# Re-planning an interleaved attention and gated-FFN kernel: plan constants, cut layer norms, the residual add on VectorE, v loads issued from GpSimd

## Chip, cores and metric

The kernel runs on one core of one Trainium2 chip. The metric is device time in microseconds (us) of one execution. f1, f2, f3 and b5 were timed on another chip than the other experiments, each beside the kernel before; across rounds the ratios to that kernel are the fair comparison. A number called *excess* is used throughout: the starts of all matmuls are taken from the trace, and from each distance between two neighbours the streaming time is taken off (0.216 us for 512 columns, 0.056 us for 128; unrounded 0.2159 and 0.0557). What is left is time in which TensorE was waiting or half clocked. A distance is put down to the later of its two matmuls.

## The reference

Two layers, each a sliding-window attention (32 heads of 32, window of 8 keys two positions apart) and a gated feed-forward part, over 2048 tokens of width 1024 in bf16:

```python
x = A_x
x = x + attn(layernorm(x), A_wqkv, A_wo)      # softmax over 8 dilated keys per query
x = x + ffn(layernorm(x), B_w1, B_w3, B_w2)   # silu(x@w1) * (x@w3) @ w2, F = 3584
x = x + attn(layernorm(x), A_wqkv, A_wo)      # same weights again
x = x + ffn(layernorm(x), B_w1, B_w3, B_w2)
```

## The kernel before

The tokens are cut into four chunks of 512. For each chunk and layer there are pieces of work: the layer norm, 24 QKV projections ("Q", 8 matmuls each), 16 products q*k on VectorE ("P"), each followed by a small reduction over the head dimension on TensorE ("R", 4 matmuls of 128 columns), a softmax ("S"), 16 weighted sums over v on VectorE ("V"), the output projection ("W"), then gate and up projections ("GU") and the down projection ("W2"). A planner in the kernel gives each piece a length, goes through time, and emits the pieces in the order of its plan; the engines then take their instructions in program order.

```python
T_LN, LAT_LN = 7.8, 4.5     # a layer norm is one block of 7.8 us on VectorE
LAT_QP = 7.0                # from a projection's end to the first product that uses it
LAT_VW = 9.0                # from the attention's end to its output projection
...
def ln_emit(c):             # one block: statistics, power, normalise, transpose, four times
    for j in range(4):
        ...  nc.vector.bn_stats ... nc.gpsimd.tensor_tensor(pow) ... nc.vector.scalar_tensor_tensor
        nc.scalar.activation(out=xn[:], in_=xc[:, j, :], func=ACTF.Identity, scale=rstd[:], bias=nmr[:])
        for kt in range(KT):
            nc.tensor.transpose(tp[:, kt, :], xn[:, P * kt:P * (kt + 1)], ident[:])
        nc.scalar.copy(out=xnT[:, :, P * j:P * (j + 1)], in_=tp[:])
...
def vl_emit():              # v loads: 4 DMAs, one buffer, issued by SyncE
    for j in range(4):
        nc.sync.dma_start(out=v2[32 * j:32 * (j + 1), :, :], in_=...)
...
def w_emit(n, j):           # output projection; the residual comes in by an identity matmul
    for ft in range(NFT):
        nc.tensor.matmul(ps[:], lhsT=oT[...], rhs=wo_sb[...], start=(ft == 0), stop=False)
    nc.tensor.matmul(ps[:], lhsT=ident[:], rhs=xs, start=False, stop=True)
    nc.scalar.copy(out=xs, in_=ps[:])
```

## Time and profile before

| | before |
|---|---|
| median of 6 runs | 1786.07 us (1782.42 to 1786.47) |
| span of the profiled run | 1780.7 us |
| matmuls, and their pure streaming | 8512, 1673.7 us |
| before the first matmul / after the last | 10.0 / 6.0 us |
| excess | 90.8 us, of it 42.2 between 120 and 360 us |

The slices of the page, the stretches and the order of matmuls near 280 us are shown in the prediction below. TensorE's waits over the whole span (total us, times, longest), first row:

```profile
PE Lps L306 <- DVE prod L290: 33.6, 17, 3.4
```

`Lps` is the accumulator of the reductions R and `prod` the VectorE product that each needs.

### The profile page before, as it was taken

The numbers are of one execution on the slowest core, as the hardware profiler recorded it, in microseconds if no ns is written. First come the engines' busy times: TensorE is split into PE (matmuls) and PEld (weight loads), VectorE is DVE, ScalarE is ACT, GpSimd is POOL, SyncE is SP. The second block draws the span as 40 slices with busy tenths as digits, with TensorE's granted clock in tenths as the row PEclk, the third lists the DMA queues.
The fourth block names the chain that finished last, engine by engine and source line by source line (L and its number), as shares of the span: only waits on it lengthen the run. The fifth ranks groups of instructions, "written<-read, shape, count | busy, mean of one in ns | idle before, by whom it ended". The sixth has DMA issues, their size and how long they took to land.

```text
span 1780.7 us, 21604 instructions
## 1 busy us (share of the span) xinstructions
PE 1698.8 (95%) x8512; PEld 812.4 (46%) x8512; DVE 1083.5 (61%) x1669; ACT 569.0 (32%) x855; POOL 41.5 (2%) x82
## 2 busy tenths in 40 slices
PE   6998994999999999999999999999999999999998
PEld 3544542444444444444444445444454444444443
DVE  5685599965688456925678256783278733333334
ACT  5442430422322334223342334322342233222221
POOL 2000000100000000000000000000000000000000
PEclk9999996999999999999999999999999999999999
DMA  9979496366346387563965459554694635546452
GB/s 298 242 234 234 149 265 144 98 169 196 97 142 170 115 249 175 148 166 126 256 166 146 139 165 238 160 167 127 206 246 131 188 112 173 153 142 189 144 160 76
DMA packets 453622, 307.13 MB, mean 172 GB/s; under 512 B 92048, under 2 KB 419728, under 8 KB 453520
## 3 DMA queue, kind: packets, MB, share of 16 engines
q1 hardware_dynamic: 453520, 305.75, 60.9%
q8 instruction: 66, 1.08, 0.3%
q14 instruction: 36, 0.29, 0.1%
HBM read 267.49 MB, written 38.22 MB: 172 GB/s over the span
## 4 chain that ended last, share of the span: by engine, by line
PE 80%; DVE 13%; DMA 3%; ACT 2%; issue 1%; POOL 0%; SPq 0%; DVEq 0%; ACTq 0%; POOLq 0%
PE mm L433 20%; PE mm L429 20%; PE mm L459 18%; PE mm L214 14%; PE mm L390 5%; DVE prod L286 3%; DVE prod L290 2%; DMA k<-Kd 2%; DVE pvtd L362 2%; DVE o L363 2%; PE tp L180 1%; DMA Kd<-qkvb 1%; PE Lps L306 1%; DVE acc L466 1%; DVE stats L168 1%
## 5 line engine op out<-in xcount | busy, mean ns | idle before, releaser
L429 PE MATMUL mm<-xnT,wb 128*128 128x512 bf16 x1792 | 424.8, 379 | 2.2 <-DVE acc L466 2.1
L433 PE MATMUL mm<-xnT,wb 128*128 128x512 bf16 x1792 | 424.2, 379 | 0.0
L459 PE MATMUL mm<-wb,hT 128*128 128x512 bf16 x1792 | 401.3, 380 | 11.2 <-DVE acc L466 9.8
L214 PE MATMUL mm<-xnT,wb 128*128 128x512 bf16 x1536 | 347.9, 382 | 4.0 <-ACT qkvb L216 4.0
L439 DVE TENSOR_TENSOR hT<-ub,sg 128x512 bf16<-128x512 bf16 x224 | 94.4, 422 | 376.1 <-ACT ub L438 376.1
L436 ACT ACTIVATE sg<-mm 128x512 bf16<-128x512 f32 x224 | 134.0, 598 | 500.5 <-PE mm L429 487.7
L459 PEld LDWEIGHTS <-hT 128*128 128x128 bf16 x1792 | 174.7, 98 | 220.7 <-issue 16.5
L433 PEld LDWEIGHTS <-wb 128*128 128x128 bf16 x1792 | 175.1, 98 | 209.9
L429 PEld LDWEIGHTS <-wb 128*128 128x128 bf16 x1792 | 173.9, 98 | 205.9 <-issue 3.2
L468 DVE TENSOR_TENSOR acc<-mm,acc 128x512 f32<-128x512 f32 x320 | 213.5, 686 | 65.4 <-PE mm L459 64.6
L214 PEld LDWEIGHTS <-wb 128*128 128x128 bf16 x1536 | 163.5, 109 | 157.8 <-issue 9.3
L286 DVE TENSOR_TENSOR prod<-q,k 128x2048 bf16<-128x2048 bf16 x128 | 153.4, 1218 | 131.3 <-DMA k<-Kd 85.9
L438 ACT CAST ub<-mm 128x512 bf16<-128x512 f32 x224 | 131.2, 586 | 239.8 <-PE mm L433 239.7
L216 ACT CAST qkvb<-mm 128x512 bf16<-128x512 f32 x192 | 111.8, 587 | 250.3 <-PE mm L214 247.3
L363 DVE TENSOR_TENSOR o<-o,pvtd 128x2048 bf16<-128x2048 bf16 x112 | 136.6, 1220 | 1.9
L362 DVE TENSOR_TENSOR pvtd<-attn,v 128x2048 bf16<-128x2048 bf16 x112 | 136.6, 1219 | 1.4
L290 DVE TENSOR_TENSOR prod<-prod 128x1024 bf16<-128x1024 bf16 (+1 forms) x256 | 131.4, 550 | 1.6
L390 PE MATMUL mm<-wo_sb,oT 128*128 128x512 bf16 x512 | 122.2, 382 | 0.0
L168 DVE BATCH_NORM_STATS2 stats<-x 128x6 f32<-128x512 bf16 x128 | 84.4, 673 | 43.0 <-ACT x L393 40.8
L177 ACT ACTIVATE xn<-x,nmr,rstd 128x1024 bf16<-128x1024 bf16 x64 | 79.9, 1251 | 47.6 <-DVE nmr L174 35.6
L306 PE MATMUL Lps<-prod,Zsel 128*128 128x128 bf16 x512 | 48.4, 228 | 33.9 <-DVE prod L290 33.6
L390 PEld LDWEIGHTS <-oT 128*128 128x128 bf16 x512 | 50.2, 99 | 59.5 <-issue 2.2
(39 smaller groups left out, 507.1 us busy)
## 6 DMA issues: line engine op xcount, KB each, us to landing
wb<-in_B_w_dram SPq DMA_DIRECT2D x336, 512.0 KB, 4.3
wb<-in_A_wqkv_dram SPq DMA_DIRECT2D x96, 512.0 KB, 5.1
v<-Vd SPq DMA_DIRECT2D x32, 284.0 KB, 6.3
k<-Kd SPq DMA_DIRECT2D x16, 526.0 KB, 4.5
Qd<-qkvb SPq DMA_DIRECT2D x16, 512.0 KB, 4.4
q<-Qd SPq DMA_DIRECT2D x16, 512.0 KB, 4.2
Kd<-qkvb SPq DMA_DIRECT2D x16, 512.0 KB, 4.4
Vd<-qkvb SPq DMA_DIRECT2D x16, 512.0 KB, 5.2
```

The source lines that it names most:

```text
L214: nc.tensor.matmul(ps[:], lhsT=wb[:, kt % (KT // 2), c_lo:c_hi:c_st], rhs=st["xnT"][:, kt, :], start=(kt == 0), stop=(kt == KT - 1))
L286: nc.vector.tensor_tensor(out=prod[:], in0=in0, in1=in1, op=ALU.mult)
L290: nc.vector.tensor_tensor(out=prod[:, 0:g], in0=prod[:, 0:g], in1=prod[:, g:2 * g], op=ALU.add)
L362: nc.vector.tensor_tensor(out=tmp[:], in0=a_b, in1=vv, op=ALU.mult)
L363: nc.vector.tensor_tensor(out=o2[:, dsl, :], in0=o2[:, dsl, :], in1=tmp[:], op=ALU.add)
L390: nc.tensor.matmul(ps[:], lhsT=oT[:, ft, P * j:P * (j + 1)], rhs=wo_sb[:, ft, 512 * n:512 * (n + 1)], start=(ft == 0), stop=False)
L429: nc.tensor.matmul(g_ps[:], lhsT=w1b[:, kt, lo:lo + P], rhs=xnT[:, kt, :], start=(kt == 0), stop=(kt == KT - 1))
L433: nc.tensor.matmul(u_ps[:], lhsT=w3b[:, kt, lo:lo + P], rhs=xnT[:, kt, :], start=(kt == 0), stop=(kt == KT - 1))
L436: nc.scalar.activation(out=sg[:], in_=g_ps[:], func=ACTF.Silu)
L438: nc.scalar.copy(out=ub[:], in_=u_ps[:])
L459: nc.tensor.matmul(ps[:], lhsT=hT[:, fi, P * j:P * (j + 1)], rhs=w2b[:, fi % 2, 512 * n:512 * (n + 1)], start=(k == 1), stop=(k == nmm))
L468: nc.vector.tensor_tensor(out=ac, in0=ps[:], in1=ac, op=ALU.add)
```

## The change

The intent is to have TensorE wait less early on and to take work from it. Five things are done at once: two latencies of the plan are raised, the layer norm is cut into twelve pieces (four of each kind) that the planner places singly, with the transposes' TensorE time now in the plan (its own plan constants and two small buffers change with it), the residual is added by VectorE, the v loads are issued from GpSimd, and layer norms are kept in the order of their stages. Cut to its core:

```diff
+V2_DMA = "gpsimd"
+LN_SPLIT = False
+A3_RES_PE = False
+W2_INTERLEAVE = False
-T_LN = 7.8
-LAT_LN = 4.5
-LAT_QP = 7.0
+T_LN = 1.95
+LAT_LN = 1.5
+LAT_QP = 13.0
-LAT_VW = 9.0
+LAT_VW = 25.0
...
-    def ln_emit(c):
+    def build_ln(name, c, st, x_deps):
+        def stats_emit(j): ...
+        def norm_emit(j): ...
+        def tr_emit(j): ...
+        for j in range(4):
+            sp_ = Pc(f"LN {name} {j}", "dve", T_LN, ...)
+            np_ = Pc(f"LNn {name} {j}", "pe", 0.0, ...)
+            tp_ = Pc(f"LNt {name} {j}", "pe", KT * T_MM128 + 0.1, ...)
...
-                nc.sync.dma_start(out=v2[32 * j:32 * (j + 1), :, :],
+                v2_dma.dma_start(out=v2[32 * j:32 * (j + 1), :, :],
...
-            nc.tensor.matmul(ps[:], lhsT=ident[:], rhs=xs, start=False, stop=True)
-            nc.scalar.copy(out=xs, in_=ps[:])
+                nc.vector.tensor_tensor(out=xs, in0=ps[:], in1=xs, op=ALU.add)
...
+        if i > 0:
+            stg[2].deps.append((stages[i - 1][2], 0.0))
```

The three flags that are off leave the corresponding parts as they were.

More of the change, by code (lines that the diff above doesn't have):

```diff
@@ L25 @@
 T_MM128 = 0.057
-T_LN = 7.8
-LAT_LN = 4.5
-LAT_QP = 7.0
+T_LN = 1.95
+LAT_LN_POW = 1.4
+LAT_LN_NRM = 1.4
+LAT_LN = 1.5
+LAT_QP = 13.0
 MARGIN_R = 2.0
-LAT_VW = 9.0
+LAT_VW = 25.0
 T_SOFTMAX = 5.6
@@ L120 @@
     nc.sync.dma_start(out=wo_sb[:], in_=A_wo.rearrange("(ft p) n -> p ft n", p=P))
+    v2_dma = {"sync": nc.sync, "gpsimd": nc.gpsimd, "scalar": nc.scalar}[V2_DMA]
     def load_w(src_ap, shape):
@@ L159, in xnt_free, with stats_emit @@
         return None if rel.end is None else rel.end + 0.3
-    def ln_emit(c):
-        xc = x_c[c]
-        xnT = work.tile([P, KT, CH], BF16, name="xnT", tag="xnT", bufs=XNT_BUFS)
-        for j in range(4):
+    def build_ln(name, c, st, x_deps):
+        def stats_emit(j):
+            if j == 0:
+                st["xnT"] = work.tile([P, KT, CH], BF16, name="xnT", tag="xnT", bufs=XNT_BUFS)
+            xc = x_c[c]
             stats = small.tile([P, 2, 6], F32, name="stats", tag="stats", bufs=3)
@@ L169, in ln_emit @@
             nc.vector.bn_aggr(out=mv[:], in_=stats[:])
-            rstd = small.tile([P, 1], F32, name="rstd", tag="rstd", bufs=3)
-            nmr = small.tile([P, 1], F32, name="nmr", tag="nmr", bufs=3)
+            rstd = small.tile([P, 1], F32, name="rstd", tag="rstd", bufs=4)
+            nmr = small.tile([P, 1], F32, name="nmr", tag="nmr", bufs=4)
             nc.vector.tensor_scalar_add(out=rstd[:], in0=mv[:, 1:2], scalar1=EPS)
@@ L175, in ln_emit, with norm_emit, tr_emit @@
                                            op0=ALU.mult, op1=ALU.mult)
+            st[("ln", j)] = (rstd, nmr)
+        def norm_emit(j):
+            rstd, nmr = st.pop(("ln", j))
             xn = work.tile([P, D], BF16, name="xn", tag="xn", bufs=2)
-            nc.scalar.activation(out=xn[:], in_=xc[:, j, :], func=ACTF.Identity, scale=rstd[:], bias=nmr[:])
+            nc.scalar.activation(out=xn[:], in_=x_c[c][:, j, :], func=ACTF.Identity, scale=rstd[:], bias=nmr[:])
+            st[("xn", j)] = xn
+        def tr_emit(j):
+            xn = st.pop(("xn", j))
             tp = psum.tile([P, KT, P], BF16, name="tp", tag="tp", bufs=1)
@@ L180, in ln_emit @@
                 nc.tensor.transpose(tp[:, kt, :], xn[:, P * kt:P * (kt + 1)], ident[:])
-            nc.scalar.copy(out=xnT[:, :, P * j:P * (j + 1)], in_=tp[:])
-        return xnT
+            nc.scalar.copy(out=st["xnT"][:, :, P * j:P * (j + 1)], in_=tp[:])
+        first = prev_s = prev_t = None
+        for j in range(4):
+            deps = list(x_deps) if j == 0 else [(prev_s, 0.0)]
+            sp_ = Pc(f"LN {name} {j}", "dve", T_LN, lambda j=j: stats_emit(j), deps=deps,
+                     extra=(xnt_free if j == 0 else None))
+            dve_urg.append(sp_)
+            np_ = Pc(f"LNn {name} {j}", "pe", 0.0, lambda j=j: norm_emit(j),
+                     deps=[(sp_, LAT_LN_POW if LN_SPLIT else 0.0)])
+            pe_small.append(np_)
+            tdeps = [(np_, LAT_LN_NRM if LN_SPLIT else 0.0)] + ([(prev_t, 0.0)] if prev_t is not None else [])
+            tp_ = Pc(f"LNt {name} {j}", "pe", KT * T_MM128 + 0.1, lambda j=j: tr_emit(j), deps=tdeps)
+            pe_small.append(tp_)
+            first = first or sp_
+            prev_s, prev_t = sp_, tp_
+        return first, prev_t
     QKV_BLOCKS = ((0, 0), (1, 0), (0, 1), (1, 1), (2, 0), (2, 1))
@@ L189, in build_attn @@
         st = {}
-        ln = Pc(f"LN A{li}.{c}", "dve", T_LN, lambda: st.__setitem__("xnT", ln_emit(c)), deps=x_deps, extra=xnt_free)
-        dve_urg.append(ln)
+        ln, ln_done = build_ln(f"A{li}.{c}", c, st, x_deps)
         big = []
@@ L235, in build_attn @@
                 p = Pc(f"Q A{li}.{c} b{bi}.{fi}", "pe", KT * T_MM, lambda bi=bi, fi=fi: q_emit(bi, fi),
-                       deps=[(ln, LAT_LN)] if (bi == 0 and fi == 0) else [], wloads=wl)
+                       deps=[(ln_done, LAT_LN)] if (bi == 0 and fi == 0) else [], wloads=wl)
                 big.append(p)
@@ L259, in vl_emit @@
                 vbase = Vt[0:1, col:col + 1].offset
-                nc.sync.dma_start(out=v2[32 * j:32 * (j + 1), :, :],
-                                  in_=bass.AP(Vt.tensor, vbase, [[vpitch, D], [1, P + HALO]]))
+                v2_dma.dma_start(out=v2[32 * j:32 * (j + 1), :, :],
+                                 in_=bass.AP(Vt.tensor, vbase, [[vpitch, D], [1, P + HALO]]))
             st["v2"] = v2
@@ L390, in w_emit @@
                 nc.tensor.matmul(ps[:], lhsT=oT[:, ft, P * j:P * (j + 1)], rhs=wo_sb[:, ft, 512 * n:512 * (n + 1)],
-                                 start=(ft == 0), stop=False)
-            nc.tensor.matmul(ps[:], lhsT=ident[:], rhs=xs, start=False, stop=True)
-            nc.scalar.copy(out=xs, in_=ps[:])
+                                 start=(ft == 0), stop=(ft == NFT - 1 and not A3_RES_PE))
+            if A3_RES_PE:
+                nc.tensor.matmul(ps[:], lhsT=ident[:], rhs=xs, start=False, stop=True)
+                nc.scalar.copy(out=xs, in_=ps[:])
+            else:
+                nc.vector.tensor_tensor(out=xs, in0=ps[:], in1=xs, op=ALU.add)
             if n == 1 and j == 3:
@@ L400, in build_attn @@
                 deps = [(lastv, LAT_VW)] if lastw is None else [(lastw, 0.0)]
-                lastw = Pc(f"W A{li}.{c} {n}.{j}", "pe", (NFT + 1) * T_MM, lambda n=n, j=j: w_emit(n, j), deps=deps)
+                lastw = Pc(f"W A{li}.{c} {n}.{j}", "pe", (NFT + (1 if A3_RES_PE else 0)) * T_MM,
+                           lambda n=n, j=j: w_emit(n, j), deps=deps, dve_cost=(0.0 if A3_RES_PE else 0.78))
                 pe_small.append(lastw)
-        return big, lastw
+        return big, lastw, ln
     def build_ffn(last, c, x_deps):
         st = {}
-        ln = Pc(f"LN B{int(last)}.{c}", "dve", T_LN, lambda: st.__setitem__("xnT", ln_emit(c)), deps=x_deps,
-                extra=xnt_free)
-        dve_urg.append(ln)
+        ln, ln_done = build_ln(f"B{int(last)}.{c}", c, st, x_deps)
         groups = [list(range(g0, min(g0 + FB_GROUP, NFB))) for g0 in range(0, NFB, FB_GROUP)]
@@ L482, in build_ffn, with mk_gu, mk_w2 @@
         gu_last = {}
-        def add_gu(fb):
-            for fi in range(4):
-                wl = [lambda fb=fb, hf=fi // 2: gu_wload(fb, hf)] if fi % 2 == 0 else []
-                p = Pc(f"GU B{int(last)}.{c} {fb}.{fi}", "pe", 2 * KT * T_MM, lambda fb=fb, fi=fi: gu_emit(fb, fi),
-                       deps=[(ln, LAT_LN)] if (fb == 0 and fi == 0) else [], dve_cost=T_DVE_GU, wloads=wl)
-                big.append(p)
-                gu_last[fb] = p
-        lastp = [None]
-        def add_w2(gi):
+        lastp = [None]
+        def mk_gu(fb, fi):
+            wl = [lambda fb=fb, hf=fi // 2: gu_wload(fb, hf)] if fi % 2 == 0 else []
+            p = Pc(f"GU B{int(last)}.{c} {fb}.{fi}", "pe", 2 * KT * T_MM, lambda fb=fb, fi=fi: gu_emit(fb, fi),
+                   deps=[(ln_done, LAT_LN)] if (fb == 0 and fi == 0) else [], dve_cost=T_DVE_GU, wloads=wl)
+            gu_last[fb] = p
+            return p
+        def mk_w2(gi):
             fbs = groups[gi]
+            res = []
             for j in range(4):
@@ L501, in add_w2 @@
                            deps=[(gu_last[fbs[-1]], 2.0)] if (j == 0 and n == 0) else [], dve_cost=T_DVE_W2, wloads=wl)
-                    big.append(p)
-                    lastp[0] = p
-        pend = None
+                    res.append(p)
+            return res
+        pend = []
         for gi, fbs in enumerate(groups):
-            for i, fb in enumerate(fbs):
-                add_gu(fb)
-                if i == 0 and pend is not None:
-                    add_w2(pend)
-                    pend = None
-            pend = gi
-        add_w2(pend)
+            gus = [mk_gu(fb, fi) for fb in fbs for fi in range(4)]
+            if W2_INTERLEAVE:
+                per = -(-len(pend) // max(1, len(gus) - 1)) if pend else 0
+                for i, g_ in enumerate(gus):
+                    big.append(g_)
+                    if i < len(gus) - 1:
+                        for _ in range(per):
+                            if pend:
+                                big.append(pend.pop(0))
+                big += pend
+            else:
+                big.append(gus[0])
+                big += pend
+                big += gus[1:]
+            pend = mk_w2(gi)
+        big += pend
+        lastp[0] = pend[-1]
         ln.rel = gu_last[NFB - 1]
-        return big, lastp[0]
+        return big, lastp[0], ln
     X0 = []
@@ L521 @@
     b3 = [build_ffn(True, c, [(a1[c][1], 1.0)]) for c in range(NCH)]
+    stages = [a0[c] for c in range(NCH)]
     for c in range(NCH):
-        pe_big += a0[c][0]
-    for c in range(NCH):
-        pe_big += b1[c][0]
+        stages.append(b1[c])
         if c >= 1:
-            pe_big += a1[c - 1][0]
-    pe_big += b3[0][0]
-    pe_big += a1[NCH - 1][0]
-    for c in range(1, NCH):
-        pe_big += b3[c][0]
+            stages.append(a1[c - 1])
+    stages.append(b3[0])
+    stages.append(a1[NCH - 1])
+    stages += [b3[c] for c in range(1, NCH)]
+    for i, stg in enumerate(stages):
+        pe_big += stg[0]
+        if i > 0:
+            stg[2].deps.append((stages[i - 1][2], 0.0))
     pe_t = dve_t = 0.0
@@ L555, with why @@
         cd = cand(dve_urg, dve_chain, dve_i, dve_t)
-        assert cp is not None or cd is not None, "planner deadlock"
+        if cp is None and cd is None:
+            def why(q):
+                return [d.name for d, _ in q.deps if d.end is None] + (["extra"] if q.extra and q.extra() is None else [])
+            msg = []
+            if big_i < len(pe_big):
+                msg.append(f"big {pe_big[big_i].name} <- {why(pe_big[big_i])}")
+            if dve_i < len(dve_chain):
+                msg.append(f"dve {dve_chain[dve_i].name} <- {why(dve_chain[dve_i])}")
+            msg += [f"small {q.name} <- {why(q)}" for q in pe_small[:3]] + [f"urg {q.name} <- {why(q)}" for q in dve_urg[:3]]
+            raise AssertionError("planner deadlock: " + "; ".join(msg))
         sp = max(pe_t, cp[0]) if cp else None
@@ L565 @@
                 dve_urg.remove(p)
-                ln_placed.append(p)
+                if p.extra is not None:
+                    ln_placed.append(p)
             else:
@@ L589 @@
         if DBG is not None:
-            DBG.append(f"{start:9.2f} {p.end:9.2f} {'DVE' if use_dve else 'PE '} {p.name}")
+            DBG.append(f"{start:9.2f} {p.end:9.2f} {'DVE' if use_dve else 'PE '} {p.name} @prio {tc.cur_priority}")
         p.emit()
```

## The prediction

> **What bounds the kernel now.** I read the page's busy shares first, then its slices, then the stretches between places where the slices change, then the order of matmuls inside the worst stretch, and last the groups of the lines that the change touches. The slices:
>
> ```profile
> PE   6998994999999999999999999999999999999998
> DVE  5685599965688456925678256783278733333334
> PEclk9999996999999999999999999999999999999999
> ```
>
> A slice is 44.5 us. TensorE is full except in slices 0, 3 and 6, and in slice 6 it is also half clocked. VectorE is full in the same slice 6. So there are two regimes: after some 320 us TensorE alone sets the end; before that something holds it up. The stretches (busy us of each engine, then the clock granted):
>
> ```profile
> 160.00:240.00 80.00, 73.96 (x401) 37.75 (x400) 50.74 (x72) 31.39 (x48) 2.19 (x4) 0.96 0.78 213
> 240.00:320.00 80.00, 56.20 (x279) 27.36 (x278) 74.90 (x96) 15.23 (x25) 0.00 (x0) 0.83 0.62 158
> 320.00:900.00 580.00, 570.32 (x2884) 271.45 (x2883) 391.51 (x615) 188.26 (x284) 16.60 (x25) 1.00 0.60 166
> ```
>
> Busy is not speed on this engine, so I also took the starts of all 8512 matmuls from the trace. Back to back, a 512-column one starts every 0.216 us and a 128-column one every 0.056 us. There are 7488 and 1024 of them: 1616.7 + 57.0 = 1673.7 us of pure streaming. The first starts at 10.0 us, 6.0 us follow the last, and the spacings beyond the two pitches add up to 90.8 us; the four make the span of 1780.7. Those 90.8 us lie so: 13.2 in the first 40 us, 7.6 from 40 to 120, 9.6 from 120 to 240, 30.4 from 240 to 320, 2.2 from 320 to 360, and 27.7 over the remaining 1420 us, of which nothing after 1480. The 30.4 are these (TensorE in order of time):
>
> ```profile
> 278.28 1.89 PE L429 MATMUL mm<-xnT,wb 128*128 128x512 bf16 x8
> 280.00 1.89 PE L433 MATMUL mm<-xnT,wb 128*128 128x512 bf16 x8
> 284.81 0.72 PE L306 MATMUL Lps<-prod,Zsel 128*128 128x128 bf16 x8 [2.92 <-DVE prod L290]
> 288.96 1.01 PE L306 MATMUL Lps<-prod,Zsel 128*128 128x128 bf16 x8 [3.43 <-DVE prod L290]
> ...
> 308.57 3.13 PE L390 MATMUL mm<-wo_sb,oT 128*128 128x512 bf16 x8
> ```
>
> TensorE takes its matmuls in program order. From 281 to 308 us the next ones are the score reductions of chunk 2, each behind a VectorE product; gate matmuls that need nothing (they run until 430 us) and the output projection of chunk 1, whose input landed at 292 us, stand behind them in the queue. The program order is made from a plan written in the kernel, and the plan believed VectorE was further on. I built the plan of the kernel before: it ends chunk 1's attention at 227.8 us and starts TensorE's projections at 12.3 us; the trace has 277.6 and 25.8. Taking off the 13.5 us of late start, VectorE is 36 us behind plan, and TensorE lost 9.6 + 30.4 = 40 us there. I read this as one debt: each us that VectorE lags the plan is a us that TensorE waits, once. VectorE in turn was idle for TensorE (columns: total, times, longest; window 40 to 320 us):
>
> ```profile
> DVE prod L286 <- PE Lps L306: 26.6, 4, 13.7
> DVE prod L286 <- DMA k<-Kd: 22.9, 2, 21.5
> DVE stats L168 <- ACT x L393: 14.1, 5, 6.6
> ```
>
> and the longest of these, 13.7 us, ends at 163 us behind a run of QKV matmuls.
>
> **What the Trainium skill says.** "TensorE: Matmul & The Clock Gate", section "Wait — 56ns, not 53.3ns?": warm matmuls follow each other in 215.7 and 55.6 ns; the trace agrees (0.216, 0.056). Its section "Part 1: The HAM clock gate" says an idle array falls to half clock; the trace shows it, 0.83 mean from 240 to 320 us. "DMA: Bandwidth & Descriptors", section "Issuing engines are not separate DMA queues": another issuing engine only saves sequencer time, so moving the v loads to GpSimd buys no bandwidth; no run so far shows it. "SBUF — State Buffer", section "SBUF: two separate sides": a GpSimd-issued DMA needs its descriptors written by GpSimd, which a VectorE operation in a 2-port mode locks out; it counts two-input tensor operations, nearly all that VectorE does here, as harmless to that. The trace before has no such DMA, so neither is tested.
>
> **The change, part by part.**
>
> The residual of the output projection leaves TensorE and ScalarE and becomes one VectorE add:
>
> ```profile
> L392 PE MATMUL mm<-x,ident 128*128 128x512 bf16 x64 | 24.3, 379 | 0.0
> L393 ACT CAST x<-mm 128x512 bf16<-128x512 f32 x64 | 37.1, 585 | 79.1 <-PE mm L392 79.1
> L466 DVE TENSOR_TENSOR acc<-mm,x 128x512 f32<-128x512 f32 x64 | 41.4, 680 | 2.1 <-PE mm L459 2.1
> ```
>
> 64 matmuls of 0.216 us are 13.8 us, no idle lies before them, so all of it comes off. 64 ScalarE copies (37 us) go as well, on an engine that is 32% busy: nothing. 64 adds come to VectorE; the third row is the same shape, so 64 x 0.68 = 43.5 us. VectorE is busy 391 of 580 us later on, so they hide there; the 8 adds of chunk 0 (5.4 us) fall in the stretch that VectorE sets, and may cost 2 us.
>
> The layer norm is cut from one block per chunk into statistics, normalisation and transposes of each 128 rows, placed singly. At the start, two chunks' norms run before the first projection: 8 groups at 2.11 us each, ScalarE's pace (1.25 normalisation, 1.01 copy), from 10.0 to 25.8 us. By my hand reading of the new placement chunk 0 is complete after the sixth or seventh group: 2 to 4 us, I take 2.5. At 98 us a block's transposes held TensorE 4.0 us; cut up I expect 3 of them back. Later norms show holes of 1 to 1.8 us each at their transposes, some 8 us in all; I take 3.
>
> The plan's latencies become truer: attention end to projection 25 us instead of 9 (the trace has 14.5, 21 and up to 49 us to the landing of its input), projection end to first product 13 instead of 7 (the trace has 9.5), and the transposes' TensorE time, 512 x 0.056 = 29 us, enters the plan for the first time. The v loads leave the SyncE queue, where three of the four for chunk 1 held back others until 164 us and a k load until 174.7 us. All this aims at the 40 us debt. I can't work out the new order without building it; I choose that about 24 of the 40 go and 16 stay, since the load latencies and the order in which SyncE serves them remain uncertain.
>
> The v loads are 4 DMAs of 1024 pieces of 284 B each per attention. GpSimd also computes the norm's power (64 x 0.6 us), strictly after whatever stands in its queue; v loads and the norm for two stages on are planned at the same moment (the plan has them 1.6 to 2.8 us apart four times). I charge 2 us.
>
> Sum: -13.8 - 2.5 - 3 - 3 - 24 + 2 + 2 = -42.3 us; 1786 - 42 = 1744. The numbers look tuned together, which I weigh with another 4 us: **1740 us**.
>
> **Rivals.** First, the debt stays: the real order is still off from VectorE's pace, perhaps because the later output projection delays the norm of the next layer. For it: the 22.9 us of k loads and the true data dependence remain. Against: VectorE has about 66 idle us from 40 to 280 us that a better order can use. It would leave 1740 + 24 = 1764. Second, GpSimd becomes the hidden bound: if a v load takes 10 us of descriptors per DMA, 40 us stand in front of a norm's power, VectorE's next operation waits behind it, and chunk 0's attention starts late (its v is ready at 87 us, used at 106, a slack of 19). For it: nothing here shows the rate. Against: the norms concerned are needed 40 to 145 us later. It would give 1760 to 1800. Third, everything works and the debt is gone: 10 + 1660 + 6 of floor plus 11 at the start and about 23 later: 1710.
>
> **Range and chances.** 2% faster needs below 1751, that is 35 us saved; 18 are nearly sure without the debt (13.8 + 2.5 + part of the rest), so the debt has to give 17 of its 40. I hold that for likely. Range 1705 to 1768; faster 0.70, same 0.27, slower 0.03.
>
> **What would show it.** Right: no matmul of the projection reads the residual; TensorE has 8448 matmuls; the spacings beyond pitch fall from 90.8 to near 60, mostly in 160 to 320 us; the half clock there shrinks; first projection matmul at 22 to 24 us. Wrong: score reductions still waiting for VectorE in a row near 280 us (first rival), VectorE or ScalarE waiting for the power on GpSimd, or v loads landing over 20 us after issue (second), new waits of TensorE on VectorE's residual adds for PSUM buffers.

## The result

| | before | after |
|---|---|---|
| median | 1786.37 us (16 runs) | 1722.79 us (8 runs) |
| span of the profiled run | 1780.7 | 1722.0 |
| matmuls, streaming | 8512, 1673.7 us | 8448, 1659.9 us |
| before the first / after the last | 10.0 / 6.0 us | 10.3 / 6.4 us |
| excess | 90.8 us | 45.2 us |

The ratio is 0.9643 (95% interval 0.9633 to 0.9653). A ratio is the mean time of the one kernel's fast runs over that of the other's of the same rounds, so not quite the ratio of the medians. The changed kernel is 63.6 us faster; between the two profiled runs it is 58.7 us: 13.8 of streaming and 45.6 of excess are gone, 0.7 came in at the two ends.

The changed kernel's slices (43 us each, busy tenths):

```profile
PE   5999899999999999999999999999999999999998
DVE  5577896799589379835689357893378752333333
PEclk9999999999999999999999999999999999999999
```

The dent of slice 6 and its half clock are gone. The stretches of the changed kernel say the same (busy us of TensorE, weight loads, VectorE, ScalarE, GpSimd, then granted clock, DMA share, GB/s):

```profile
160.00:240.00 80.00, 73.36 (x400) 37.41 (x399) 65.85 (x93) 27.75 (x40) 2.73 (x4) 0.98 0.77 217
240.00:320.00 80.00, 76.86 (x386) 35.74 (x384) 65.88 (x96) 16.02 (x26) 4.25 (x6) 1.00 0.63 168
320.00:900.00 580.00, 575.26 (x2954) 275.43 (x2952) 427.47 (x672) 187.84 (x273) 31.04 (x38) 1.00 0.60 172
```

From 240 to 320 us TensorE went from 56.2 to 76.9 busy us. What fills it is seen in TensorE's order of time, the changed kernel at the same point of its work (attention of chunk 1 just ended; L337 is R, L462 and L466 are gate and up, L421 is W):

```profile
283.12 0.39 PE L337 MATMUL Lps<-prod,Zsel 128*128 128x128 bf16 x4
283.35 1.89 PE L462 MATMUL mm<-xnT,wb 128*128 128x512 bf16 x8
285.07 1.89 PE L466 MATMUL mm<-xnT,wb 128*128 128x512 bf16 x8
286.80 1.89 PE L462 MATMUL mm<-xnT,wb 128*128 128x512 bf16 x8
288.53 1.89 PE L466 MATMUL mm<-xnT,wb 128*128 128x512 bf16 x8
290.25 0.39 PE L337 MATMUL Lps<-prod,Zsel 128*128 128x128 bf16 x4
...
303.79 8.80 PE L421 MATMUL mm<-wo_sb,oT 128*128 128x512 bf16 x40
```

Before, thirteen reductions stood one behind the other here (284.8 to 308.6 us), at VectorE's pace. Now gate and up projections, which wait for nothing, lie between them. It is not that VectorE got quicker: it ends chunk 1's attention at 268.7 us instead of 277.6, 8.9 us earlier, while the excess from 120 to 360 us fell by 28.7 (42.2 to 13.5). TensorE's waits on the products over the whole span:

```profile
PE Lps L337 <- DVE prod L321: 10.1, 6, 3.4
```

33.6 us became 10.1.

**A count that can be read without running.** In the compiled program order of TensorE I counted the R's that directly follow another R, with no other matmul between: 34 of 128 before, 18 after. VectorE makes a product and its two sums in some 2.07 us, TensorE reduces it in 0.22, so each R of such a run can cost up to about 1.8 us. The count serves as a yardstick for the excess at R's in the experiments, not for the time.

### The profile page after: what moved, and what is told of

Same layout as the page of the kernel before. It is cut to its first block, busy times and chain, and to the rows that moved or that the text cites. A ratio compares the mean times of both kernels' runs of the same rounds, so it can differ in the third digit from the quotient of the medians.

```text
span 1722.0 us, 21416 instructions
## 1 busy us (share of the span) xinstructions
PE 1678.3 (97%) x8448; PEld 803.3 (47%) x8448; DVE 1117.3 (65%) x1733; ACT 533.0 (31%) x791; POOL 70.7 (4%) x114
## 2 busy tenths in 40 slices
DMA packets 423412, 307.11 MB, mean 178 GB/s; under 512 B 59280, under 2 KB 387472, under 8 KB 423312
## 3 DMA queue, kind: packets, MB, share of 16 engines
q0 software_dynamic: 3072, 9.31, 3.1%
## 4 chain that ended last, share of the span: by engine, by line
PE 75%; DVE 18%; DMA 3%; ACT 3%; issue 1%; SPq 0%; POOL 0%; DVEq 0%; ACTq 0%; POOLq 0%
PE mm L466 17%; PE mm L462 17%; PE mm L492 17%; PE mm L245 16%; PE mm L421 6%; DVE pvtd L393 4%; DVE o L394 4%; DVE acc L501 2%; DVE prod L317 2%; PE Lps L337 1%; DVE prod L321 1%; DVE hT L472 1%; PE tp L197 1%; ACT xnT L198 1%; DVE o L390 1%
## 5 line engine op out<-in xcount | busy, mean ns | idle before, releaser
L462 PE MATMUL mm<-xnT,wb 128*128 128x512 bf16 x1792 | 425.4, 379 | 0.5 <-DVE acc L501 0.5
L466 PE MATMUL mm<-xnT,wb 128*128 128x512 bf16 x1792 | 423.5, 379 | 0.0
L466 PEld LDWEIGHTS <-wb 128*128 128x128 bf16 x1792 | 175.3, 98 | 210.8
L462 PEld LDWEIGHTS <-wb 128*128 128x128 bf16 x1792 | 173.2, 98 | 200.3 <-issue 1.4
L321 DVE TENSOR_TENSOR prod<-prod 128x1024 bf16<-128x1024 bf16 (+1 forms) x256 | 135.1, 550 | 2.3
L421 PE MATMUL mm<-wo_sb,oT 128*128 128x512 bf16 x512 | 114.7, 379 | 0.7 <-DVE x L427 0.7
L427 DVE TENSOR_TENSOR x<-mm,x 128x512 bf16<-128x512 f32 x64 | 43.7, 685 | 61.0 <-PE mm L421 61.0
L182 POOL TENSOR_TENSOR rstd<-rstd,neghalf 128x1 f32<-128x1 f32 x64 | 43.0, 673 | 968.5 <-DVE rstd L181 682.2
```

The lines of the kernel that those rows point to most:

```text
L321: nc.vector.tensor_tensor(out=prod[:, 0:g], in0=prod[:, 0:g], in1=prod[:, g:2 * g], op=ALU.add)
L421: nc.tensor.matmul(ps[:], lhsT=oT[:, ft, P * j:P * (j + 1)], rhs=wo_sb[:, ft, 512 * n:512 * (n + 1)], start=(ft == 0), stop=(ft == NFT - 1 ...
L462: nc.tensor.matmul(g_ps[:], lhsT=w1b[:, kt, lo:lo + P], rhs=xnT[:, kt, :], start=(kt == 0), stop=(kt == KT - 1))
L466: nc.tensor.matmul(u_ps[:], lhsT=w3b[:, kt, lo:lo + P], rhs=xnT[:, kt, :], start=(kt == 0), stop=(kt == KT - 1))
```

## The experiments

All outputs are right. "Excess" is split into what lies before an R and the total of the run. Each number is of one kernel's profiled run; times are medians, ratios are to the kernel before in the same rounds.

| run | time us | ratio | R behind R | excess at R | excess in all |
|---|---|---|---|---|---|
| kernel before | 1786.4 | 1 | 34 | 40.0 | 90.8 |
| changed kernel | 1722.8 | 0.9643 | 18 | 12.7 | 45.2 |
| e1: residual back on TensorE | 1747.9 | 0.9786 | 15 | 15.8 | 56.4 |
| e2: v loads back on SyncE | 1804.4 | 1.0106 | 44 | 58.8 | 125.1 |
| e3: old latencies | 1783.0 | 0.9995 | 35 | 59.1 | 103.5 |
| e4: norm in a block | 1730.6 | 0.9691 | 20 | 12.4 | 53.8 |
| f1: changed, TensorE's order forced to the plan | 1740.1 | 0.9739 | 8 | 10.4 | 60.4 |
| f2: f1 with v loads on SyncE | 1748.8 | 0.9790 | 8 | 8.4 | 69.0 |
| f3: before, order forced to the plan | 1824.0 | 1.0211 | 14 | 14.7 | 133.0 |
| b5: before + latencies + v loads | 1733.8 | 0.9705 | 19 | 5.8 | 41.5 |
| b1: before + latencies | 1801.1 | 1.0085 | 40 | 48.6 | 109.4 |
| b3: before + v loads | 1770.1 | 0.9915 | 31 | 36.6 | 80.5 |
| g0: changed, quicker start | 1717.8 | 0.9621 | 18 | 13.6 | 39.5 |
| g1: g0, two constants by the count | 1722.3 | 0.9646 | 13 | 14.9 | 43.7 |

The theory going in was that of the prediction: a plan nearer to the truth removes the early debt. The first rival was that SyncE's queue, freed of the v loads, did it; the second that the cut layer norm did.

### Undoing one part of the changed kernel

**e1, the residual back on TensorE**

```diff
-A3_RES_PE = False
+A3_RES_PE = True
```

> The changed kernel with the residual back on TensorE (64 identity matmuls and 64 ScalarE copies), nothing else undone. If the residual is worth its streaming alone: 13.8 us slower than the changed kernel (1722.8), so about 1736.6, with TensorE's spacings beyond pitch unchanged near 45 us. If the VectorE adds cost something in the stretch that VectorE sets, less than 10 us slower. If the moved adds also shift the plan for the better, more than 18 us slower and the 240 to 360 us stretch gets back over 10 us of excess.

Measured: 25.1 us slower than the changed kernel. 13.8 of it is the streaming of 64 matmuls; the excess rose by 11.2, most of it between 240 and 640 us. Of the third case the time came true (over 18 us slower), the place only in part: from 240 to 360 us 7.1 us came back (3.9 to 11.0), not over 10. The part also moves the plan, and that is worth about as much again here.

**e2, the v loads back on SyncE**

```diff
-V2_DMA = "gpsimd"
+V2_DMA = "sync"
```

> The changed kernel with the v loads back on the SyncE queue; the plan is the same to the last piece. Plan theory: within 3 us of the changed kernel (1720 to 1726). Rival (the SyncE queue was the cause): over 15 us slower, with SyncE waiting at the v loads for VectorE and k loads issued late again around 170 us.

Measured: 81.6 us slower, and slower than the kernel before. My theory had said within 3 us and missed by far; the rival's "over 15 us" came true, and k loads of chunk 1 did go out later (127.3 and 134.8 us, 99.9 and 114.8 in the changed kernel), though not at 170. So this run alone can't tell queue from order; f1 and f2 below do. What it shows is that the planner's plan is the same, but the compiled order is not. R's that directly follow another one are 44. TensorE's order of time in this run (L337 is R):

```profile
177.41 0.38 PE L337 MATMUL Lps<-prod,Zsel 128*128 128x128 bf16 x4 [1.69 <-DVE prod L321]
179.48 0.58 PE L337 MATMUL Lps<-prod,Zsel 128*128 128x128 bf16 x4 [1.69 <-DVE prod L321]
181.56 0.58 PE L337 MATMUL Lps<-prod,Zsel 128*128 128x128 bf16 x4 [1.49 <-DVE prod L321]
...
195.44 14.40 PE L245 MATMUL mm<-xnT,wb 128*128 128x512 bf16 x56
```

Every 2.07 us one R, and nothing between; 56 projection matmuls come behind them. TensorE's waits of this run, first row:

```profile
PE Lps L337 <- DVE prod L321: 48.6, 32, 3.3
...
PE mm L421 <- DVE x L427: 11.2, 2, 7.0
```

The R's have 46.1 of the 79.9 us of added excess. The second row is a further part: the output projection waits for VectorE's residual adds.

This run also refutes the "debt of VectorE" as I had put it: VectorE ended chunk 1's attention at 256.8 us, 11.9 us *earlier* than in the changed kernel, and yet TensorE's excess from 120 to 240 us was 30.8 against 9.6.

**e3, the old latencies**

```diff
-LAT_QP = 13.0
-LAT_VW = 25.0
+LAT_QP = 7.0
+LAT_VW = 9.0
```

> The changed kernel with the two latencies of the plan as before (7 and 9 us for 13 and 25). Plan theory: the debt returns; the excess spacings between 120 and 360 us grow from 13.5 to 30 to 40 us and the time to 1738 to 1750. Rival (the cut layer norm did it): under 5 us slower.

Measured: 60.2 us slower, nearly the kernel before. The direction is the theory's, the size is over it: excess from 120 to 360 us is 39.7, as expected, but 44 us of excess lie after 360 us, which I had not expected. For orientation only, the count of the compiled order without a run: with 9 us to the output projection alone it is 31, with 7 us to the first product alone 18. It points to the 25 us as the constant that matters, which no run tested singly.

**e4, the layer norm in one block again** (the order between the stages' norms is kept, and the plan's latency after a norm goes back with the block)

```diff
-LAT_LN = 1.5
+LAT_LN = 4.5
...
-        for j in range(4):
-            sp_ = Pc(f"LN {name} {j}", "dve", T_LN, lambda j=j: stats_emit(j), ...)
-            np_ = Pc(f"LNn {name} {j}", "pe", 0.0, lambda j=j: norm_emit(j), ...)
-            tp_ = Pc(f"LNt {name} {j}", "pe", KT * T_MM128 + 0.1, lambda j=j: tr_emit(j), ...)
+        sp_ = Pc(f"LN {name}", "dve", 4 * T_LN, block_emit, deps=list(x_deps), extra=xnt_free)
```

> The changed kernel with each layer norm again in one block of four (statistics, normalisation and transposes together, the transposes' TensorE time again outside the plan). Plan theory: the holes at later transposes come back; excess after 360 us from 10.9 to about 25 us, so 14 us slower, and a few more early on since the plan again leaves out 2.2 us of TensorE time per norm: 1735 to 1745. Rival (the cut layer norm did nearly everything): 1760 or more. If cutting does nothing: within 4 us of 1722.8.

Measured: 7.8 us slower, less than expected. The excess before transposes rose from 17.1 to 24.6 us, about the whole loss. By time, the excess after 360 us rose from 11.0 to 21.1, nearly all of it between 360 and 640 us; after 640 us it is 4.5 against 4.2. So the holes that the kernel before has at transposes late in the run did not come back with the block.

The four losses add up to 175 us where the whole change gained 64. The parts do not add; they act together through the order.

### Taking the order out of the compiler's hands

For f1 to f3, TensorE's pieces are tied one behind the other in the order of the plan (an order of issue, no wait on data):

```diff
-        p.emit()
+        if not use_dve and pe_seen[1] is not None:
+            with tc.issue_after(pe_seen[1]):      # last TensorE instruction of the piece before
+                p.emit()
+        else:
+            p.emit()
```

**f1, the changed kernel so forced**

> The changed kernel with TensorE's program order tied to the plan, piece behind piece (order only, no new waits on data), so that the compiler's list scheduler can't reorder it. Score reductions that directly follow another reduction, with no other matmul between: 8 (changed kernel 18, the kernel before 34). If runs of such reductions are what the early stall is (1.75 us each), their excess falls below 10 us and the time is within 10 us of 1722.8 or better; if the plan's order without the scheduler is worse elsewhere (matmuls in order behind an operand that is late), it shows as waits before projections or norm transposes and the time is 1730 to 1760.

**f2, the same with v loads on SyncE**

> The same forced order (TensorE's instructions are the same to the last one), v loads on SyncE instead of GpSimd. Order theory (the 82 us that the v loads on SyncE cost came from the program order made under them): within 6 us of the forced kernel with v loads on GpSimd. Queue theory (the SyncE queue itself, held by the v loads, starves TensorE of weights when it runs): over 20 us slower than it, with TensorE waiting for weight loads.

Measured: f1 is 1740.1 us, 17 slower than the changed kernel, as its second case had it; f2 is 1748.8, 8.7 slower than f1. They were run on another chip. TensorE's instructions of f1 and f2 are the same to the last one. With TensorE's order free, the same move of the v loads cost 81.6 us. So the queue's own part was 8.7 us here, and the rest of the 81.6, up to nine tenths, comes with the program order, if the queue costs the same under both orders (the orders of VectorE and SyncE still differ between f1 and f2). The 8.7 is of the size of these rows of TensorE's waits, f1 and then f2:

```profile
PE mm L245 <- DMA wb<-in_A_wqkv_dram: 3.4, 3, 1.7
```

```profile
PE mm L245 <- DMA wb<-in_A_wqkv_dram: 8.6, 2, 7.1
```

TensorE waits 5.2 us longer for QKV weights. The order theory expected within 6 us, the queue theory over 20; 8.7 is near the first. f1 also shows the price of the plan's raw order: its excess at R is 10.4, but that at norm transposes is 30.7 against 17.1 in the changed kernel. The pass that orders the instructions at build is useful there and harmful at the R's of the kernel before.

**f3, the kernel before so forced**

> The kernel before with TensorE's order tied to its own plan: 14 reductions directly behind another one instead of 34. If runs of reductions are the cause: their excess of 40 us falls by 20 or more, time below 1770. If the plan's short latencies are the deeper cause: the excess moves to waits before the output projection (planned 9 us after the attention's end, its operand lands 14 to 21 us after) and the time stays within 1 per cent of the kernel before or gets worse.

Measured: 1824.0 us. It was run on another chip. The excess at R did fall, from 40.0 to 14.7, as the first case says, but the time got worse by 38 us:

```profile
PE tp L180 <- ACT xnT L181: 57.6, 46, 2.4
...
PE Lps L306 <- DVE prod L290: 10.3, 6, 2.3
```

The excess moved to the norm's transposes (78.7 us, 23.6 before), not to the output projection (5.8), as the second case had it. TensorE waits for ScalarE between the transposes. That the block norm can't stand in plan order because its transposes' time is missing in the plan is my reading, not tested.

### Single parts and a pair on the kernel before

**b1, the latencies alone**

```diff
-LAT_QP = 7.0
-LAT_VW = 9.0
+LAT_QP = 13.0
+LAT_VW = 25.0
```

> The kernel before with the new latencies alone, v loads still on SyncE. Its program order has 40 reductions directly behind another one (34 before, 19 with the v loads moved as well). Run theory: no gain, 1785 to 1805, excess at reductions of 40 to 60 us. If the latencies alone are the cure: below 1760.

Measured: 15.9 us slower than the kernel before of the same rounds, as the count of 40 had said.

**b3, the v loads on GpSimd alone**

```diff
-                nc.sync.dma_start(out=v2[32 * j:32 * (j + 1), :, :],
+                nc.gpsimd.dma_start(out=v2[32 * j:32 * (j + 1), :, :],
```

> The kernel before with the v loads on GpSimd alone, old latencies. 31 reductions directly behind another one. Run theory: little gain, 1770 to 1787, most of the excess at reductions stays. If freeing SyncE is the cure by itself: below 1755.

Measured: 15.1 us faster; the excess at R is still 36.6. This is within what was expected.

**b5, both**

> The kernel before with two parts only: the new latencies (13 and 25) and the v loads on GpSimd. The reductions directly behind another one are 19 in its program order, as in the changed kernel (18). Run theory: nearly all of the debt goes, excess 240 to 360 us below 8 us, time 1787 less 28 to 36, so 1750 to 1760; the rest of the 64 us is the residual (13.8 or more) and the cut norm (8 to 17).

Measured: 1733.8 us, 52.3 us faster, more than the 28 to 36 expected. It was run on another chip. So +15.9 and -15.1 become -52.3 together. With a block norm and the residual still on TensorE this pair has 41.5 us of excess, less than the changed kernel's 45.2: excess at R is 5.8, and after 360 us 8.4. TensorE's waits on the products in b5:

```profile
PE Lps L306 <- DVE prod L290: 4.9, 3, 3.4
```

The pair is what removes the stall, early and late. Set beside e4 and e1, which add the residual alone and the cut norm alone to it (both also keep the order between norms, which b5 does not):

| | norm in a block | norm cut |
|---|---|---|
| residual on TensorE | 1733.8 (b5) | 1747.9 (e1) |
| residual on VectorE | 1730.6 (e4) | 1722.8 (changed) |

Neither of the two is worth much alone on top of the pair (3.2 gained, 14.1 lost); together they give 11.0. The 3.2 is not clear of the noise: the ratios, 0.9705 and 0.9691, have intervals that overlap. And the 14.1 can be the cut norm's or the order's between norms.

### A quicker start

In the changed kernel all eight norm groups of chunks 0 and 1 still precede the first projection, at ScalarE's pace:

```profile
23.04 1.01 PE L197 MATMUL tp<-ident,xn 128*128 128x128 bf16 x8 [1.10 <-ACT xnT L198]
25.15 1.01 PE L197 MATMUL tp<-ident,xn 128*128 128x128 bf16 x8 [1.10 <-ACT xnT L198]
26.71 5.48 PE L245 MATMUL mm<-xnT,wb 128*128 128x512 bf16 x17 [0.55 <-DMA wb<-in_A_wqkv_dram]
```

and the first weights land only then. **g0** loads chunk 0's rows, then weights, then the other rows, and makes chunk 1's norm wait for the first projection in the plan:

```diff
+    for q in pe_big[:5]:                 # first weights right after chunk 0's rows
+        for f in q.wloads: f()
+        q.wdone = True
+    ... zero padding, rows of chunks 1 to 3; output weights after the twelfth big piece
-            stg[2].deps.append((stages[i - 1][2], 0.0))
+            stg[2].deps.append((stages[i - 1][2], 0.0) if i > 1 else (a0[0][0][1], 0.0))
```

> The changed kernel with a quicker start: rows of chunk 0, then the first weights, then the rest of the rows, the output weights later; the norm of chunk 1 only after chunk 0's first projection. Same count of adjacent reductions (18). The start is set by ScalarE, 8 norm groups of 2.11 us before the first projection; with 4 of them the first projection starts near 19 us instead of 26.7, and the whole shifts: 1714 to 1718 against 1722.8 for the changed kernel. If the weights are what sets the start, or the time is given back at the first attention: 1720 to 1726.

Measured: 1717.8 us, ratio 0.9621. The start of g0:

```profile
16.95 1.01 PE L192 MATMUL tp<-ident,xn 128*128 128x128 bf16 x8 [1.10 <-ACT xnT L193]
19.06 8.65 PE L240 MATMUL mm<-xnT,wb 128*128 128x512 bf16 x32 [1.10 <-ACT xnT L193]
```

The first projection starts 7.6 us earlier, and the excess of the first 40 us fell from 14.4 to 8.7, which is the whole gain of 5 to 6 us between the two traces (some 4 us by the ratios). This is the fastest kernel.

**g1** takes g0 and two constants with the lowest count among those tried:

```diff
-LAT_QP = 13.0
-MARGIN_R = 2.0
+LAT_QP = 9.0
+MARGIN_R = 4.0
```

> The same quicker start with two constants of the plan chosen by the count of adjacent reductions in the program order (13 instead of 18): 9 for 13 us from projection to first product, 4 for 2 us of margin before a reduction. If the count tells the time: 5 x 1.75 = 9 us under the run before it in this list at most, so 1706 to 1716. If the count misses what matters: no faster than it.

Measured: 1722.3 us, 4.5 slower than g0, with excess at R of 14.9 against 13.6. Five adjacent R's fewer brought nothing. In all fourteen kernels the count tells two groups apart: 31 to 44 go with 36 to 59 us of excess at R, 8 to 20 with 6 to 16. Inside the lower group it does not rank them: an R behind an R costs nothing where its product is long done, and in f1 two waits make 9.5 of the 10.4 us. Nor does it tell the time: the slowest kernel, f3, has 14.

## Why the prediction was right, and where not

The predicted 1740 was 17 us too slow, inside the range of 1705 to 1768; faster was the likeliest class. Part of this was luck. The 24 us of the largest term were chosen, not worked out, and the prediction saw nothing that would tell the changed kernel from e2, which has the same plan and took 1804 us: which order the build makes of the plan decided it. The terms add up as written, but for one slip: 2% below 1786 is 1750, not 1751. By its own steps:

- *The residual, -13.8.* The streaming went exactly as worked out: 64 matmuls fewer. The VectorE add took 0.69 us, as the row of the same shape had said:

```profile
L427 DVE TENSOR_TENSOR x<-mm,x 128x512 bf16<-128x512 f32 x64 | 43.7, 685 | 61.0 <-PE mm L421 61.0
```

  "All of it comes off" was too simple: on top of the pair it gave 3.2 us with a block norm (b5 to e4, not clear of the noise) and 25.1 with a cut one (e1 to the changed kernel), because it also changes the order.
- *The start, -2.5.* Failed. The hand reading of the placement had six or seven groups before the first projection; eight precede it, it starts at 26.7 instead of 25.8 us, and excess up to 40 us rose from 13.2 to 14.4. g0 shows what it takes.
- *The hole at 98 us, -3.* Excess from 40 to 120 us fell by 1.2. "Transposes held TensorE" was loose: the trace has the 4.0 us as a projection that waits for ScalarE's copies of earlier ones (`qkvb`), which ran after the norm's work on ScalarE. That hole is gone, but an R now waits 3.1 us near 103 us for a product whose k load landed at 104.4.
- *The early debt, -24 of 40.* From 120 to 360 us the excess fell from 42.2 to 13.5, by 28.7. The size was right. The reason was half right: it is a matter of program order, but "each us that VectorE lags the plan" is not the rule (in e2 VectorE is the earlier through chunk 1, and TensorE loses more). What costs is a run of reductions with no other matmul between. And I took the program order for the plan's order; at build another order is made from it, in which 34 R's adjoin where the plan has 14.
- *Later norms, -3.* Mis-sized: after 360 us the excess fell from 27.7 to 11.0, by 16.7. At the transposes themselves it fell by 5.3 (7.5 to 2.2), not far from the 3; the rest is mostly 6.8 at R's (8.3 to 1.5) and 5.1 at the down projections (9.7 to 4.6), for which the prediction had no term. The cut norm is not needed for it: b5, with the block and the residual on TensorE, has 8.4 there. But with the residual on VectorE the block has 21.1 (e4), so its worth depends on the other parts. This term is most of what the prediction lacked; the 4 us added for "tuned together" was in its direction.
- *VectorE adds and GpSimd, +2 each.* TensorE's waits for the adds, a sign of being wrong by the prediction, are 1.5 us in all (two waits; 11.2 us in e2). GpSimd was not seen as a cost: VectorE's waits for its power fell from 18.8 to 7.0 us. The v loads kept GpSimd 25.3 us in all:

```profile
L291 POOL DMA_DIRECT2D v<-Vd x32 | 25.3, 797 | 380.6 <-DMA Vd<-qkvb 247.1 <-DMA wb<-in_A_wqkv_dram 72.3 <-DMA wb<-in_B_w_dram 52.8
```

  0.8 us per DMA, landing 7.7 us after issue in the median and 11.6 at most, against 6.3 and 9.2 from SyncE. The prediction's second rival had feared 10 us of descriptors per DMA.

Of the prediction's rivals the first (the debt stays) is out, the second too. The third (everything works, 1710) was nearer than I weighed it.

On the skill's pages: "DMA: Bandwidth & Descriptors", section "Issuing engines are not separate DMA queues", says another issuer only saves sequencer time. With TensorE's order fixed this is close to what f1 and f2 show, 8.7 us over 32 loads; with the order free, so that it moved with the edit, the same edit was worth 81.6 us in the changed kernel and 15.1 in the kernel before. "SBUF — State Buffer", section "SBUF: two separate sides", tells of a probe in which `tensor_tensor` on VectorE did not stall a GpSimd-issued DMA, and marks its reason for this as inferred. 25 of the 32 loads here were issued during such operations; each of the 32 held GpSimd for 0.78 to 0.95 us, and 0.78 is also what one took at 156.8 us, when VectorE was idle. This agrees.

**What stays open.** Why the build places R's side by side when the v loads are on SyncE, or when the latencies are short, is not shown: the runs show the orders and their cost, not the reason for the choice. Whether the 25 us alone would do without the 13 was not run. The order between the stages' norms was never undone by itself. And f1 and f2 fix TensorE's order only, so that a share of the 73 us between 81.6 and 8.7 may belong to the other engines' orders, or to a queue that costs more under e2's order than under the plan's.

## What to carry to other kernels

Where one engine takes small pieces at another's pace, look in its program order for runs of such pieces with nothing between: each costs the other engine's pace, and work that could fill the gap stands behind. Check the order that was compiled, not the plan that was written, and check it again after every edit, since a moved DMA or a changed constant can reorder everything; parts of such a change can't be judged one by one. Before believing that a queue was the cause, fix the order and move the queue alone.

## What the Trainium skill lacked or had wrong

- *DMA: Bandwidth & Descriptors*: it has no time for generating many small descriptors on GpSimd. Here a DMA of 1024 pieces of 284 B held GpSimd for 0.8 us and landed in 7.7 us (median), 1.4 us later than from SyncE.
- *DMA: Bandwidth & Descriptors*: it says for GpSimd-issued DMAs that a packet has preferably up to 4096 B; it does not say that the same copy from SyncE is cut otherwise. Packets of the kernel before and of the changed one:

```profile
DMA packets 453622, 307.13 MB, mean 172 GB/s; under 512 B 92048, under 2 KB 419728, under 8 KB 453520
```

```profile
q0 software_dynamic: 3072, 9.31, 3.1%
DMA packets 423412, 307.11 MB, mean 178 GB/s; under 512 B 59280, under 2 KB 387472, under 8 KB 423312
```

  32,768 packets under 512 B (32 loads of 1024 pieces) became 3072 of about 3.0 KB (9.31 MB over 3072). I had not expected this. f1 and f2 differ in the same way (423,412 and 453,620 packets), so what it saves there is part of the 8.7 us between them; how much was not tested.
- *Issuing engines are not separate DMA queues* (same page): true of the transfers, but it lets a reader expect nothing of moving loads. The runs show 81.6 us where the program order follows the move and 8.7 where TensorE's order is held.
- No page has the cost of adjacent small matmuls that each wait for VectorE. Here it is up to some 1.8 us for each; in the kernel before the excess at reductions, adjacent or not, is 40.0 us.
